# Turning the softmax weights as fp32r through a second tile at the same address

## The chip, the core and the metric

The kernel runs on one core of a Trainium2 chip. The metric is the device time of one execution in microseconds; the kernel before takes 804.97 us, the median of three runs from 804.18 to 805.74.

## What is computed

Three pieces follow each other. Attention with 2 batches, 8 heads, 576 rows and 64 columns a head keeps the 32 largest scores of every row. Its result, 1152 rows of 512, goes through a mixture of four experts, and that through a gated block:

```python
scores = scale * q @ k.T                       # 576 x 576 for each of 16 heads
kth = np.partition(scores, -32, axis=-1)[..., -32:-31]
attn = softmax(np.where(scores >= kth, scores, -1e9))
x = (attn @ v) as 1152 x 512
out = sum(p[:, e:e + 1] * (relu(x @ w1[e]) @ w2[e]) for e in range(4))   # F = 1024
out = (out @ w_a) * (out @ w_b) @ w_out        # 1536 columns between
```

## The kernel before

The rows are cut into nine tiles of 128 rows (eight of whole blocks, and one, MIX, of the 64 rows left over in each batch). The tiles form four groups of 1, 2, 3 and 3. Attention goes through 36 steps: for every group its four pairs of heads, and for every pair the tiles of the group. Steps 0 to 3 are of group 0, 4 to 11 of group 1, 12 to 23 of group 2 and 24 to 35 of group 3.

One step handles one tile and two heads. TensorE makes the scores; ScalarE moves them to SBUF (L905); VectorE finds the 32 largest of each row with eight MAX8 (L933) and six MATCH_REPLACE8 (L941), the replacements going into a buffer `e`. Then comes the softmax: GpSimd makes the ends (L958), ScalarE marks the kept scores (L964), GpSimd subtracts (L968), ScalarE takes the exponential (L972), GpSimd and VectorE make the reciprocal of the sum (L977 and L980), and ScalarE scales (L983). The softmax weights stand in `e`, of which there are three buffers, 1152 words each, inside the region `low`. In `weigh` (from L1015) TensorE turns them, four 128x128 transposes for one head and five for the other, all from the one line L573; ScalarE moves them to SBUF (L1050), and after the last tile of a pair they are multiplied with the values, from which `xs`, the experts' input, comes (L1084 and L1086).

Steps 0 to 23 turn `e` as float32. Steps 24 to 35 (the table `MOVED`) first copy both halves of `e` by a transfer into one of two buffers `er` of type fp32r in the region `big`, and turn those as fp32r.

The experts' work on a group needs all four pairs of that group. Its first layer has as moving operand 256 columns for group 1 and 384 for groups 2 and 3 (an experts' input of two or three tiles), its second layer 512. Weights are split in two fp32r parts by ScalarE (L1107) and GpSimd or VectorE (L1108). The sums of a group (L1205) are turned back in `replace` (transposes on L573 of float32, L1308, L1312).

All work is recorded as operations with an engine, an estimated duration, a priority key, the operations and the buffers that it waits for. A planner (`Plan.best`) simulates 42 orders from its own table of durations and keeps one; the instructions are then written out engine by engine in that order. Each engine runs its own instructions strictly in that order, so one instruction that waits holds up all that stand behind it on its engine. A changed duration, wait or buffer anywhere lets the planner place everything anew.

Of the kernel before, what the change touches and what calls it, by code (L numbers as in the profile page):

```python
# [9 lines left out]
F32 = mybir.dt.float32  # L10
F32R = mybir.dt.float32r
# [18 lines left out]
AHEAD = 2.4  # L30
OPERANDS = 3.0
STORED, STORE_AT, STORE_KEY = 3, 10, 2.5
MOVED = (*range(24,36),)

# [4 lines left out]
class Slots:  # L39
# [10 lines left out]
    def tile(self, need=0.0):  # L50
        t = Buffer(self, need)
        self.queue.append(t)
        return t
# [23 lines left out]
class Buffer:  # L77
    def __init__(self, slots, need):
        self.slots, self.need, self.slot, self.users = slots, need, None, 0

    @property
    def ap(self):
        a = self.slots.aps[self.slot]
        return a[0][a[1]] if isinstance(a, tuple) else a


class Op:
# [296 lines left out]
TURN_R, TURN_F, TOP, REPLACE = 88, 109, 662, 732  # L384
# [18 lines left out]
def body(tc, q, k, v, probs, w1, w2, wa, wb, wo, out):  # L403
    nc = tc.nc

    wa, wb, wo = (w.bitcast(U32) for w in (wa, wb, wo))
    B, H, S, D = q.shape
    E, DM, F = w1.shape
# [3 lines left out]
    M4 = S // 128  # L412
    MAIN = M4 * 128
# [7 lines left out]
    sb = stack.enter_context(tc.tile_pool(name="sb", bufs=1))  # L421
# [36 lines left out]
    identr = const("identr", [128, 128], F32R)  # L458
    ident = identr.bitcast(F32)
# [13 lines left out]
    big = Region("big", 10752, F32R)  # L473
# [8 lines left out]
    big.at = 0  # L482
    ers = big.slots("er", 2, 2 * S)
    ers.rank = 0.5
    mid = Region("mid", 4 * 2048 + 5 * 768, F32)
    wides = mid.slots("wide", WIDE, 2048)
    mid.again(F32R)
# [4 lines left out]
    first_ = Region("lowa", 4 * 2 * S + 4 * S, F32)  # L492
    pts = first_.slots("pt", 4, 2 * S)
    ss = first_.slots("s", 4, S)
    low = Region("low", 9228 + 3 * DM, F32)
    kraws = low.slots("kraw", 2, 2 * M4 * D)
    vts = low.slots("vt", 4, 2 * M4 * D)
    qraws = low.slots("qraw", 1, 2 * 3 * D)
    es = low.slots("e", 3, 2 * S)
    m8s = low.slots("m8", 2, 2 * TOPK)  # L500
    endss = low.slots("ends", 2, 4)
    sumss = low.slots("sums", 2, 2)
    hfs = low.slots("hf", 2, 512)
    krraws = kraws
    low.at = 9228
    yps = low.slots("yp", 1, DM)
    pws = low.slots("pw", 1, 1024)
    low.again()
    low.at = 9228
    ys = low.slots("y", 1, 3 * DM)  # L510

    first_.again(F32R)
# [3 lines left out]
    raw.again()  # L516
    ress = [raw.slots("res", 8, DM)]
    low.again()
    ress.append(low.slots("res2", 1, DM))
    draws = low.slots("draw", 2, 1024)  # L520
    dcs = low.slots("dc", 2, 512)
    vvs = low.slots("vv", 2, 2048)
    tps = [low.slots("tp", 2, 4 * 320), rest.slots("tpr", 1, 4 * 320)]
    taken_ = []
    ydone, ahead = {}, {}

# [36 lines left out]
    def gpsimd(hold, emit, key, after, tiles, lag=55):  # L563
        return plan.add("POOL", hold, emit, key, after, tiles, lag=lag, port=True)

    def tensor(hold, emit, key, after, tiles):
        return plan.add("PE", hold, emit, key, after, tiles, lag=165)
# [2 lines left out]
        nc.tensor.matmul(out, l, r, **kw)  # L570

    def tr(out, a, i):
        nc.tensor.transpose(out, a, i)  # L573

    def token_rows(t, rows):

# [22 lines left out]
    ready = gpsimd(1900, consts, -1e6, (), ())  # L599
# [417 lines left out]
    def weigh(pair, i, ed, n):  # L1017
# [15 lines left out]
        ke = -3000 if fast else -900  # L1033
        for j in range(2):

            at = atts.tile(kt)

            def turn(j=j, at=at):
                a = (at.ap if f is e else at.ap.bitcast(F32R)).rearrange("p b n -> p (b n)")
                if j:  # L1040
                    tr(a[:, MAIN - 128:MAIN], f.ap[:, MAIN:MAIN + 128], idt)
                for m in range(M4):
                    c0 = j * (S + REM) + m * 128
                    tr(a[:, j * MAIN + m * 128:j * MAIN + (m + 1) * 128], f.ap[:, c0:c0 + 128], idt)

            hold = (M4 + j) * TURN_F if f is e else 46 + (M4 + j - 2) * 85 + 64
# [575 lines left out]
```

## Time and profile before

| what | value |
|---|---|
| median of three runs | 804.97 us (804.18 to 805.74) |
| profiled execution, from first to last instruction | 802.1 us |
| TensorE matmul busy | 777.2 us, 97% |
| VectorE busy | 731.2 us, 91% |
| ScalarE busy | 528.6 us, 66% |
| GpSimd busy | 358.8 us, 45% |

The page gives the profiled execution no time but its span, which lies 2.9 us under the median of the runs. PE stands for TensorE's matmuls, DVE for VectorE, ACT for ScalarE, POOL for GpSimd, SP for the queue that issues transfers. A share of busy time is an average over stages with different limits, so the stages have to be read one by one; a PE that is shown busy is not always at its full rate, since the ends of matmuls are modelled.

### The profile page before, as it was taken

How to read it: one execution, taken by the hardware profiler on the slowest of the kernel's cores; microseconds unless marked ns; L12 is line 12 of the kernel's file. 1: busy time of each engine (PE TensorE's matmuls, PEld its weight loads, DVE VectorE, ACT ScalarE, POOL GpSimd, SP SyncE). 2: the span in 40 equal slices, each digit the busy share in tenths (PEclk: the TensorE clock that was granted, in tenths of full speed). 3: DMA queues.
4: the chain of work that ended last, by engine and by line, in shares of the span. 5: the costliest groups of instructions: out<-in, count | busy, mean ns of one | idle time of the engine just before them, and what ended most of it. 6: DMA issues, size and time to landing. Idle time of an engine off the chain costs nothing.

```text
span 802.1 us, 14540 instructions
## 1 busy us (share of the span) xinstructions
PE 777.2 (97%) x5221; PEld 701.1 (87%) x5221; DVE 731.2 (91%) x1430; ACT 528.6 (66%) x926; POOL 358.8 (45%) x323
## 2 busy tenths in 40 slices
PE   6699998999999999999999999999999999999998
PEld 5577776889999989999998898999888989899996
DVE  7999999999999999999996599898889998989655
ACT  5999888999898897877676566666545524242110
POOL 4645345899789856842111002332224334343120
PEclk7699999999999999999999999999999999999999
DMA  5987996867648575754444555888531322312013
GB/s 173 326 277 232 306 325 223 265 202 232 214 141 253 165 230 179 220 182 144 135 154 152 160 175 176 274 294 316 173 106 54 132 59 100 132 33 73 1 53 119
DMA packets 98008, 143.57 MB, mean 179 GB/s; under 512 B 11792, under 2 KB 66064, under 8 KB 96400
## 3 DMA queue, kind: packets, MB, share of 16 engines
q1 hardware_dynamic: 97936, 142.65, 55.5%
q8 instruction: 41, 0.67, 0.3%
q14 instruction: 31, 0.25, 0.1%
HBM read 117.46 MB, written 14.42 MB: 164 GB/s over the span
## 4 chain that ended last, share of the span: by engine, by line
PE 69%; DVE 17%; ACT 5%; DMA 3%; POOL 3%; issue 3%; SPq 0%; POOLq 0%; ACTq 0%; DVEq 0%
PE ps L570 66%; DVE low L933 7%; DVE low L941 6%; PE ps L573 3%; DMA mid<-in_moe_w_dram 1%; POOL low L968 1%; ACT mid_again L1107 1%; POOL mid_again L1108 1%; ACT lowa L905 1%; DMA big<-low 1%; DVE rest L1513 1%; ACT low L972 1%; DMA low<-in_q_dram 1%; POOL big L629 1%; DVE mid_again L1180 1%
## 5 line engine op out<-in xcount | busy, mean ns | idle before, releaser
L570 PE MATMUL ps<-mid_again 128*128 128x512 f32 x1092 | 263.0, 392 | 0.0
L570 PEld LDWEIGHTS ps<-mid_again 128*128 128x128 f32 x1092 | 201.2, 188 | 38.8
L570 PE MATMUL ps<-xs,mid_again 128*128 128x384 f32 (+1 forms) x1152 | 193.6, 320 | 0.5 <-DVE mid_again L1180 0.3
L570 PEld LDWEIGHTS ps<-xs,mid_again 128*128 128x128 f32 x1152 | 182.2, 189 | 3.2 <-issue 0.5
L933 DVE MAX8 low<-low 128x8 f32<-128x576 f32 x216 | 153.8, 745 | 0.0
L1424 POOL TENSOR_TENSOR low<-low 128x512 int32<-128x512 int32 x36 | 52.2, 1450 | 164.7 <-DVE low L1421 98.6
L1108 POOL TENSOR_TENSOR mid_again<-raw,mid_again 128x1024 fp32r<-128x1024 f32 x48 | 115.4, 2411 | 13.8 <-ACT mid_again L1107 8.2
L1107 ACT ACTIVATE mid_again<-raw 128x1024 fp32r<-128x1024 f32 x96 | 101.7, 1065 | 21.9 <-PE ps L570 14.3
L968 POOL TENSOR_TENSOR low<-lowa,low 128x576 f32<-128x576 f32 x72 | 102.0, 1433 | 28.0 <-ACT low L964 28.0
L941 DVE MATCH_REPLACE8 low<-low 128x576 f32<-128x576 f32 x144 | 106.0, 741 | 0.0
L570 PE MATMUL ps<-xs,big 128*128 128x320 f32 (+1 forms) x576 | 86.4, 297 | 0.2 <-DVE low L1513 0.2
L570 PEld LDWEIGHTS ps<-xs,big 128*128 128x128 f32 x576 | 80.3, 190 | 1.1 <-DVE low L1513 0.4
L1108 DVE TENSOR_TENSOR mid_again<-raw,mid_again 128x1024 fp32r<-128x1024 f32 x48 | 62.6, 1306 | 6.9 <-ACT mid_again L1107 6.9
L570 PE MATMUL ps<-lowa_again,big 128*128 128x320 f32 (+1 forms) x432 | 66.2, 296 | 0.9 <-ACT rest L1522 0.8
L1176 ACT ACTIVATE mid_again<-ps 128x384 fp32r<-128x384 f32 (+1 forms) x96 | 44.1, 461 | 30.1 <-PE ps L570 29.6
L570 PEld LDWEIGHTS ps<-lowa_again,big 128*128 128x128 f32 x432 | 60.7, 190 | 2.0 <-ACT rest L1522 1.1
L972 ACT ACTIVATE low<-low 128x576 f32<-128x576 f32 x72 | 56.2, 783 | 3.1 <-POOL low L968 3.0
L964 ACT ACTIVATE low<-lowa,low 128x576 f32<-128x576 f32 x72 | 53.9, 778 | 5.1 <-POOL low L958 5.1
L983 ACT ACTIVATE low<-low 128x576 f32<-128x576 f32 x72 | 53.2, 776 | 5.5 <-DVE low L980 5.4
L905 ACT ACTIVATE lowa<-ps 128x576 f32<-128x576 f32 x72 | 46.2, 655 | 15.9 <-POOL low L968 8.1
L1180 DVE SCALAR_TENSOR_TENSOR mid_again<-ps,mid_again 128x384 fp32r<-128x384 f32 (+1 forms) x96 | 48.1, 502 | 7.2 <-ACT mid_again L1176 6.9
L1516 POOL TENSOR_TENSOR low<-low 128x256 f32<-128x256 f32 (+1 forms) x30 | 28.5, 950 | 56.0 <-DVE low L1513 51.1
(122 smaller groups left out, 1189.2 us busy)
## 6 DMA issues: line engine op xcount, KB each, us to landing
raw<-in_moe_w_dram SPq DMA_DIRECT2D x116, 512.0 KB, 4.5
big<-kscr SPq DMA_DIRECT2D x20, 576.0 KB, 5.3
big<-low SPq DMA_DIRECT2D x24, 288.0 KB, 3.9
low<-in_v_dram SPq DMA_DIRECT2D x24, 256.0 KB, 4.2
low<-in_moe_w_b_dram SPq DMA_DIRECT2D x12, 512.0 KB, 3.6
low<-in_moe_w_a_dram SPq DMA_DIRECT2D x12, 512.0 KB, 3.5
low<-in_moe_w_out_dram SPq DMA_DIRECT2D x12, 512.0 KB, 4.3
wscr<-big SPq DMA_DIRECT2D x6, 1024.0 KB, 5.8
```

What stands on the lines that cost most here:

```text
L570: nc.tensor.matmul(out, l, r, **kw)
L905: S, lambda: nc.scalar.activation(s.ap.rearrange("p (c n) -> p c n", c=2), at.ap[:, :, 0:HALF], AF.Copy),
L933: 62 + 1.04 * width, lambda at=at, cs=cs: nc.vector.max(m8v()[:, x, cs], at()), key + 0.02 * r, [done],
L941: lambda at=at, cs=cs: nc.vector.match_replace(out=src[1](), in_to_replace=m8v()[:, x, cs], in_values=at(), imm_value=LOW),
L964: S, lambda x=x, s=s: nc.scalar.activation(ev(x), s.ap, AF.Relu, bias=endv()[:, x, 1:2], scale=-STEEP),
L968: pool_(S), lambda x=x, s=s: nc.gpsimd.tensor_tensor(ev(x), s.ap, ev(x), op=ALU.subtract), ks, [a], [s, ep]
L972: lambda x=x: nc.scalar.activation(ev(x), ev(x), AF.Exp, bias=endv()[:, x, 0:1], scale=scale, accum_out=sums.ap[:, x:x + 1]),
L983: S, lambda x=x: nc.scalar.activation(ev(x), ev(x), AF.Copy, scale=sums.ap[:, x:x + 1]),
L1107: hi = scalar(1024, lambda: nc.scalar.activation(u.ap[:, 0:1024], r.ap, AF.Copy), 500 + s, [ld], [u, r], sbuf=True)
L1108: sub = lambda eng: eng.tensor_tensor(u.ap[:, 1024:2048], r.ap, u.ap[:, 0:1024], op=ALU.subtract)
L1180: lambda h=h, p=p: nc.vector.scalar_tensor_tensor(h.ap[:, n:2 * n], p.ap[:, 0:n], 0.0, h.ap[:, 0:n], op0=ALU.max, op1=ALU.subtract),
L1424: return gpsimd(pool_(512), lambda: nc.gpsimd.tensor_tensor(t().bitcast(I32), fold(c.ap.bitcast(I32)), fold(lowv().bitcast(I32)), op=ALU.a ...
```

## The change

The three buffers `e` leave the region `low` and become tiles of their own, 1160 words each. Every step takes a new float32 tile in one of the three places. When the softmax weights are finished, `retype` takes a second tile of type fp32r at the same address and writes one word behind the weights with a GpSimd memset; that instruction stands for the producer of the fp32r tile. It waits for both L983 of the step, and the transposes, now fp32r in all 36 steps, wait for it. Before, the first head's transposes waited for the first L983 alone. The copies into `er` are gone, and so are those two buffers. Later users of the region `low` move to other offsets, and the buffers `draw` and `dc` of the last stage take the places of `e`. The planner's duration for a turn is now 280 and 365 ns instead of 436 and 545.

```diff
-MOVED = (*range(24,36),)
     def ap(self):
         a = self.slots.aps[self.slot]
+        if isinstance(a, Typed):
+            self.own = a.tile(F32) if self.own is None else self.own
+            return self.own[:, 0:a.words]
         return a[0][a[1]] if isinstance(a, tuple) else a
+class Typed:
+    def tile(self, dtype):
+        self.n += 1
+        return self.pool.tile([128, self.words + 8], dtype, name=f"{self.name}_{self.n}", tag=self.name)
-    ers = big.slots("er", 2, 2 * S)
-    low = Region("low", 9228 + 3 * DM, F32)
+    low = Region("low", 7180, F32)
-    es = low.slots("e", 3, 2 * S)
+    turns = [Typed(sb, f"e{i}", 2 * S) for i in range(3)]
+    es = Slots("e", turns, "e", [(i * 2 * S, (i + 1) * 2 * S) for i in range(3)])
...
-        f, idt = e, ident
-        if n in MOVED:
-
-            f, idt = ers.tile(n), identr
-            done = [load(
-                lambda j=j: f.ap[:, j * S:(j + 1) * S].bitcast(F32), lambda j=j: e.ap[:, j * S:(j + 1) * S], n + 0.1, [done[j]], [e, f], S * 512,
-            ) for j in range(2)]
+        turnable = []
+
+        def retype():
+            a = e.slots.aps[e.slot]
+            t_ = a.tile(F32R)
+            turnable[:] = t_, nc.gpsimd.memset(t_[:, a.words:a.words + 1].bitcast(F32), 0.0).ins
+
+        typed = gpsimd(90, retype, -4500, done, [e])
...
-            o = tensor(hold, turn, kt, [done[j], done[0], ready], [at, f])
+            o = tensor(46 + (M4 + j - 2) * 85 + 64, turn, kt, [typed, ready], [at, e])
```

What the planner made of it is shown at the softmax and the turn of step 23, the last step of group 2. Lines of the kernel after lie 19 further on for the steps' operations (L968 is L987, L980 is L999), 25 for the experts' (L1108 is L1133, L1312 is L1337). In the kernel after, the tiles of `e` carry their place and a serial number: step 23 is `e2_15_2673` as float32 and `e2_16_2942` as fp32r, step 24 is `e0_17_2815`, step 25 `e1_17_2910`.

GpSimd in the kernel before, from the ends of step 23 (L958) to the sums of its exponentials (L977):

```order
L958 TENSOR_TENSOR low<-low,facs 128x4
L1108 TENSOR_TENSOR mid_again<-raw,mid_again 128x1024
L968 TENSOR_TENSOR low<-lowa,low 128x576 x2
L1108 TENSOR_TENSOR mid_again<-raw,mid_again 128x1024
L977 TENSOR_SCALAR low<-low 128x2
```

GpSimd in the kernel after, from the memset of step 22 to the memset of step 23:

```order
L1048 MEMSET e1_16_2818 128x1
L977 TENSOR_TENSOR low_80<-low_80,facs_69 128x4
L1133 TENSOR_TENSOR mid_again_1275<-raw_78,mid_again_1275 128x1024
L987 TENSOR_TENSOR e2_15_2673<-lowa_79,e2_15_2673 128x576
L1133 TENSOR_TENSOR mid_again_1275<-raw_78,mid_again_1275 128x1024 x2
L987 TENSOR_TENSOR e2_15_2673<-lowa_79,e2_15_2673 128x576
L977 TENSOR_TENSOR low_80<-low_80,facs_69 128x4
L996 TENSOR_SCALAR low_80<-low_80 128x2
L987 TENSOR_TENSOR e0_17_2815<-lowa_79,e0_17_2815 128x576 x2
L1048 MEMSET e2_16_2942 128x1
```

Two more weight splits of 128x1024 stand between the two subtractions of step 23, the memset of step 22 stands ahead of its ends, and step 24's ends stand ahead of its sums.

VectorE in the kernel before, the last rows up to the reciprocal of step 23:

```order
L941 MATCH_REPLACE low<-low 128x576 x2
L933 MAX low<-low 128x8 x2
L941 MATCH_REPLACE low<-low 128x576
L1205 SCALAR_TENSOR_TENSOR low<-ps,pr,low 128x512
L941 MATCH_REPLACE low<-low 128x576
L980 RECIPROCAL low<-low 128x2
```

VectorE in the kernel after, the last rows up to the same reciprocal (L999):

```order
L1337 TENSOR_TENSOR xs_70<-ps_81,xs_70 128x2x256
L952 MAX low_80<-e0_17_2815 128x8
L952 MAX low_80<-lowa_79 128x8
L960 MATCH_REPLACE e1_17_2910<-low_80,lowa_79 128x576
L1337 TENSOR_TENSOR xs_70<-ps_81,xs_70 128x2x256
L952 MAX low_80<-lowa_79 128x8
L952 MAX low_80<-e1_17_2910 128x8
L960 MATCH_REPLACE e1_17_2910<-low_80,lowa_79 128x576
L960 MATCH_REPLACE e1_17_2910<-low_80,e1_17_2910 128x576
L999 RECIPROCAL low_80<-low_80 128x2
```

Before, step 24 was not yet through when the reciprocal came; after, step 24 is through and three replacements of step 25 and both L1312 of group 1 stand ahead of it.

TensorE in the kernel before around the turn of step 23 (the nine transposes from `low`):

```order
L570 MATMUL ps<-mid_again 128x512 x6
L570 MATMUL ps<-big 128x288 x8
L570 MATMUL ps<-mid_again 128x512 x18
L570 MATMUL ps<-xs,mid_again 128x384 x6
L573 MATMUL ps<-identr,low 128x128 x9
L570 MATMUL ps<-xs,mid_again 128x384 x6
L570 MATMUL ps<-big,qm 128x288 x8
```

TensorE in the kernel after around the same turn (`e2_16_2942`); the eight transposes from `low_80` are those of group 1's sums:

```order
L589 MATMUL ps_81<-mid_again_1275 128x512 x15
L592 MATMUL ps_81<-identr_65,e1_16_2818 128x128 x9
L589 MATMUL ps_81<-mid_again_1275 128x512 x6
L589 MATMUL ps_81<-big_76 128x288 x8
L589 MATMUL ps_81<-xs_70,mid_again_1275 128x384 x18
L592 MATMUL ps_81<-identr_65,low_80 128x128 x8
L589 MATMUL ps_81<-xs_70,mid_again_1275 128x384 x9
L592 MATMUL ps_81<-identr_65,e2_16_2942 128x128 x9
L589 MATMUL ps_81<-big_76,qm_68 128x288 x8
```

Of group 2's first layer 27 matmuls of 384 columns stand ahead of the turn instead of 6, and the eight transposes of group 1's sums, which stood behind it, stand ahead of it; all else ahead of the turn is the same in both kernels.

## Rows read from the trace of the kernel before

**Rows 1.** The page: busy time and share of the span by engine.

```profile
PE 777.2 (97%) x5221; PEld 701.1 (87%) x5221; DVE 731.2 (91%) x1430; ACT 528.6 (66%) x926; POOL 358.8 (45%) x323
```

**Rows 2.** Busy time by stretch: stretch, length, PE, PEld, DVE, ACT, POOL (instructions), clock, DMA.

```profile
60.00:135.00 75.00, 72.23 (x531) 56.33 (x531) 74.90 (x168) 65.92 (x123) 34.44 (x39) 1.00 0.87 275
160.00:285.00 125.00, 123.58 (x980) 113.15 (x979) 124.18 (x271) 114.21 (x212) 110.22 (x81) 1.00 0.67 206
285.00:420.00 135.00, 135.00 (x952) 124.19 (x953) 132.77 (x262) 105.46 (x182) 61.45 (x52) 1.00 0.54 170
420.00:802.00 382.00, 376.86 (x2258) 346.86 (x2256) 318.77 (x559) 171.57 (x274) 101.53 (x88) 1.00 0.41 137
```

**Rows 3.** The chain that ended last, 255 to 300 us: start, us, what.

```profile
270.61 0.66 DVE low L1205
...
280.90 1.46 DVE low L941 x2
...
284.15 0.69 DVE xs L1312
...
285.54 7.02 PE ps L570 x36
```

**Rows 4.** Timeline of TensorE at turns: start, us, engine, line, op, tiles, count.

```profile
87.81 1.15 PE L573 MATMUL ps<-identr,low 128*128 128x128 f32 x9
88.79 0.39 PE L570 MATMUL ps<-xf,raw 128*128 128x128 f32 x2
...
205.02 1.15 PE L573 MATMUL ps<-identr,low 128*128 128x128 f32 x9
205.92 1.40 PE L570 MATMUL ps<-mid_again 128*128 128x512 f32 x5
...
337.50 0.89 PE L573 MATMUL ps<-identr,big 128*128 128x128 f32 x9
338.23 1.16 PE L570 MATMUL ps<-mid_again 128*128 128x512 f32 x4
```

**Rows 5.** Timeline of TensorE, 268 to 293 us: step 23's turn, group 1's transposes.

```profile
273.61 1.15 PE L573 MATMUL ps<-identr,low 128*128 128x128 f32 x9
...
284.88 0.66 PE L573 MATMUL ps<-identr,low 128*128 128x128 f32 x4 [0.57 <-DVE xs L1312]
285.34 4.45 PE L570 MATMUL ps<-xs,mid_again 128*128 128x384 f32 x24
```

**Rows 6.** Timeline of GpSimd in step 23's softmax.

```profile
261.79 0.20 POOL L958 TENSOR_TENSOR low<-low,facs 128x4 f32<-128x4 f32 x1 [0.56 <-PE ps L570]
262.22 2.41 POOL L1108 TENSOR_TENSOR mid_again<-raw,mid_again 128x1024 fp32r<-128x1024 f32 x1 [0.24 <-ACT mid_again L1107]
264.58 2.82 POOL L968 TENSOR_TENSOR low<-lowa,low 128x576 f32<-128x576 f32 x2
```

**Rows 7.** Timeline of VectorE: last MAX8 and reciprocal of step 23.

```profile
260.23 1.41 DVE L933 MAX8 low<-low 128x8 f32<-128x576 f32 x2
...
271.91 0.15 DVE L980 RECIPROCAL low<-low 128x2 f32<-128x2 f32 x1
```

**Rows 8.** Instructions of one line: ns of one, min/median/max, and when.

```profile
L596 POOL MEMSET facs<- x1: 101/101/101, 2.1 to 2.1; 128x2 f32 x1
```

**Rows 9.** Last copy into `er` and the turn behind it: transfers page, chain, TensorE's timeline.

```profile
big<-low SPq DMA_DIRECT2D x24, 288.0 KB, 3.9
437.01 5.27 DMA big<-low
442.33 0.63 PE L573 MATMUL ps<-identr,big 128*128 128x128 f32 x5 [0.16 <-DMA big<-low]
```

**Rows 10.** Granted clock by stretch, and a wait that left it alone (columns as in rows 2).

```profile
20.00:30.00 10.00, 5.87 (x28) 5.11 (x29) 10.00 (x22) 9.41 (x22) 6.28 (x8) 0.50 0.90 281
130.00:140.00 10.00, 7.66 (x63) 5.24 (x63) 10.00 (x22) 8.11 (x13) 6.84 (x6) 1.00 0.53 171
135.06 0.66 PE L573 MATMUL ps<-identr,low 128*128 128x128 f32 x4 [2.35 <-ACT low L983]
```

More of the change, by code (lines that the diff above doesn't have):

```diff
@@ L79, in __init__ @@
         self.slots, self.need, self.slot, self.users = slots, need, None, 0
+        self.own = None
     @property
@@ L83, in ap, with __init__, __getitem__ @@
         a = self.slots.aps[self.slot]
+        if isinstance(a, Typed):
+            self.own = a.tile(F32) if self.own is None else self.own
+            return self.own[:, 0:a.words]
         return a[0][a[1]] if isinstance(a, tuple) else a
+class Typed:
+    def __init__(self, pool, name, words):
+        self.pool, self.name, self.words, self.n, self.last = pool, name, words, 0, None
+    def tile(self, dtype):
+        self.n += 1
+        return self.pool.tile([128, self.words + 8], dtype, name=f"{self.name}_{self.n}", tag=self.name)
+    def __getitem__(self, span):
+        if self.last is None:
+            self.last = self.tile(F32)
+        return self.last[:, span[0]:span[1]]
 class Op:
@@ L481, in body @@
     qts = big.slots("qt", 1, 2 * 3 * 128)
-    big.at = 0
-    ers = big.slots("er", 2, 2 * S)
-    ers.rank = 0.5
     mid = Region("mid", 4 * 2048 + 5 * 768, F32)
@@ L498, in body @@
     qraws = low.slots("qraw", 1, 2 * 3 * D)
-    es = low.slots("e", 3, 2 * S)
+    turns = [Typed(sb, f"e{i}", 2 * S) for i in range(3)]
+    es = Slots("e", turns, "e", [(i * 2 * S, (i + 1) * 2 * S) for i in range(3)])
+    es.rank = 0
     m8s = low.slots("m8", 2, 2 * TOPK)
@@ L504, in body @@
     krraws = kraws
-    low.at = 9228
+    low.at = 5644
     yps = low.slots("yp", 1, DM)
@@ L508, in body @@
     low.again()
-    low.at = 9228
+    low.at = 5644
     ys = low.slots("y", 1, 3 * DM)
@@ L518, in body @@
     low.again()
-    ress.append(low.slots("res2", 1, DM))
-    draws = low.slots("draw", 2, 1024)
-    dcs = low.slots("dc", 2, 512)
+    draws = Slots("draw", [(turns[i], (0, 1024)) for i in range(2)], "e", [(i * 2 * S, i * 2 * S + 1024) for i in range(2)])
+    dcs = Slots("dc", [(turns[2], (i * 512, (i + 1) * 512)) for i in range(2)], "e", [(4 * S + i * 512, 4 * S + (i + 1) * 512) for i in range(2)])
+    draws.rank = dcs.rank = 1
     vvs = low.slots("vv", 2, 2048)
     tps = [low.slots("tp", 2, 4 * 320), rest.slots("tpr", 1, 4 * 320)]
+    ress.append(low.slots("res2", 1, DM))
     taken_ = []
@@ L572, in tr @@
     def tr(out, a, i):
-        nc.tensor.transpose(out, a, i)
+        return nc.tensor.transpose(out, a, i)
     def token_rows(t, rows):
@@ L1023, in weigh @@
         (e, done), p, ptd = ed, pts.tile(n), []
-        f, idt = e, ident
-        if n in MOVED:
-            f, idt = ers.tile(n), identr
-            done = [load(
-                lambda j=j: f.ap[:, j * S:(j + 1) * S].bitcast(F32), lambda j=j: e.ap[:, j * S:(j + 1) * S], n + 0.1, [done[j]], [e, f], S * 512,
-            ) for j in range(2)]
+        turnable = []
[4 more added lines that the diff above has]
+        typed = gpsimd(90, retype, -4500, done, [e])
+        typed.port = False
         fast = n in HURRIED or n in SOONER
@@ L1038, in turn @@
             def turn(j=j, at=at):
-                a = (at.ap if f is e else at.ap.bitcast(F32R)).rearrange("p b n -> p (b n)")
+                a = at.ap.bitcast(F32R).rearrange("p b n -> p (b n)")
+                f, by = turnable
+                made = []
                 if j:
-                    tr(a[:, MAIN - 128:MAIN], f.ap[:, MAIN:MAIN + 128], idt)
+                    made.append(tr(a[:, MAIN - 128:MAIN], f[:, MAIN:MAIN + 128], identr))
                 for m in range(M4):
                     c0 = j * (S + REM) + m * 128
-                    tr(a[:, j * MAIN + m * 128:j * MAIN + (m + 1) * 128], f.ap[:, c0:c0 + 128], idt)
-            hold = (M4 + j) * TURN_F if f is e else 46 + (M4 + j - 2) * 85 + 64
-            o = tensor(hold, turn, kt, [done[j], done[0], ready], [at, f])
+                    made.append(tr(a[:, j * MAIN + m * 128:j * MAIN + (m + 1) * 128], f[:, c0:c0 + 128], identr))
+                tc.add_manual_dep(
+                    made[0].ins, by.name, mybir.DependencyInfo(mybir.DependencyClass.Sync, mybir.DependencyReason.DATA), reason="the tile's new type"
+                )
+            o = tensor(46 + (M4 + j - 2) * 85 + 64, turn, kt, [typed, ready], [at, e])
             w = MAIN + j * 128
```

## The prediction

> **What bounds the kernel now.** I read the profile from the whole to the stage. The page's first part says that TensorE is busy 97% of a span of 802.1 us and VectorE 91% [rows 1]: with 25 us of idle time on TensorE, work taken from it could shorten the kernel, if it is TensorE that the end waits for where the work is taken. So the next view is busy time by stretch [rows 2]. From 60 to 135 us VectorE is busy 74.90 of 75 us, from 160 to 285 us 124.18 of 125. It does top-8 searches and replacements there without a pause, and these set the pace at which steps are finished. TensorE is nearly full too, but has 2.8 and 1.4 us of idle time in the same stretches. From 285 to 420 us TensorE has no idle time at all, 135.00 of 135. Where does the pace change hands? The chain of work that ended last answers it [rows 3]: it runs along VectorE's searches up to the L1312 at 284.15 us, and goes over to TensorE at 284.88, to stay there but for short pieces. That is the border between groups 1 and 2. TensorE has finished what it can do for group 1, and group 2's experts need step 23, the last of their attention.
>
> So there are two stages. **Ahead of 285 us** the border is reached when VectorE has got through step 23, and time saved on TensorE becomes waiting. **Behind it** every microsecond of TensorE counts, but the turns there (steps 24 to 35) are fp32r already.
>
> **What the change takes off TensorE.** Nine float32 transposes take 0.90 us to the start of the next matmul (205.02 to 205.92), nine fp32r ones 0.73 (337.50 to 338.23) [rows 4]: 0.17 a step. Among float32 matmuls nine take 0.98 us (87.81 to 88.79) [rows 4], 0.25 over the fp32r row. For the 24 steps concerned that is 24 x 0.17 = 4.1 us, or 24 x 0.25 = 6.0. All of it lies ahead of the border. The wait of 2.35 us for an L983 at 135.06 us [rows 10] is the same situation one group earlier: there too the turn came later than TensorE could have taken it.
>
> The pages would have promised more. The Trainium skill, "FP8 and Floating Point Precision", section "TensorE Precision Notes", gives true float32 four passes through the array. By it a turn's transposes would fall to a quarter, and 24 x 0.90 x 3/4 = 16 us would go. The trace does not show that for transposes, whose rows stand at 0.90 and 0.73, and the measurement decides.
>
> **What goes with the transfers.** The 24 copies of 288 KB took 3.9 us each, the last one 5.27 us in the chain, but TensorE stood idle only 0.16 us for it [rows 9]; the others lay beside experts' matmuls in a stretch where TensorE never paused [rows 2]. I take 0.2 us. If the cover were gone it would be some 4 us for each of 12 steps; nothing in the order takes it away, since TensorE has group 2's matmuls to do all the while.
>
> **What is added.** 36 memsets of one word. The only small ones of the trace took 0.10 us [rows 8], so GpSimd gets 36 x 0.1 = 3.6 us; the bounds are 0 for one hidden and 2.41 us, a weight split, for one that must let that run out ahead of it [rows 6]. GpSimd is busy 110.22 of 125 us ahead of the border [rows 2], so the turn of a step will often wait for a split. A step's turn is not waited for in most cases; TensorE takes other work. The memset also waits for both L983, and behind it GpSimd's queue holds, in 13 of 36 places, the ends of the next step (L958). At step 23 that is the case. I take 0.1 to 0.8 us for the wait there: 0.1 for the memset, the rest for the second L983, for which the first head's turn did not wait before.
>
> **What is moved** decides. At step 23 GpSimd ran L958, one split and both subtractions in 5.6 us (261.79 to 267.40) [rows 6]. In the new order two more splits of 2.41 us stand between the subtractions, 4.8 us more. VectorE's own order follows that: ahead of step 23's reciprocal (271.91) [rows 7] now stand five more MAX8, three more replacements, one more L1205 and both L1312. Two MAX8 take 1.41 us [rows 7], two replacements 1.46, an L1205 0.66, an L1312 0.69 [rows 3]: 3.5 + 2.2 + 0.7 + 1.4 = 7.8 us; the 1.41 counts an overlap, so I take 7.5. VectorE cannot make this up, having no idle time there, and the order on an engine is fixed. The turn of step 23 began at 273.61, 1.7 us behind its reciprocal, so it should now begin near 281.
>
> TensorE gets work for this time: 21 matmuls of 384 columns that stood behind the turn, at 4.45 / 24 = 0.185 us (counting an overlap, so 0.18) [rows 5], 3.8 us; and the eight transposes of group 1's sums, two of the runs of 0.46 us (284.88 to 285.34) [rows 5], 0.9 us. Together 4.7. The rest of the 7.5 us, 2.8, is lost for good, because what is behind the turn is the same in kind and number but for these 4.7 us, and TensorE is the bound from there on. TensorE itself should be seen idle longer than 2.8 us around the border, by what it saved on the turns of steps 12 to 23 (12 x 0.17 = 2 us) and the 0.57 us below.
>
> **The sum,** against the profiled span of 802.1: +7.5 for the reciprocal of step 23, -4.7 for the work moved ahead of its turn, +0.1 to +0.8 for memset and second half (0.5 taken), -0.57 for the wait for L1312 at 284.88 [rows 5], which now falls in the longer wait, -0.2 for the transfers: 802.1 + 2.5 = 804.6. The saving on the turns stands at nothing in it. The median of the runs lies 2.9 us over the span; put on it, the same sum gives 804.97 + 2.5 = **807.5 us**. The memset between its ends (0 and 2.41) moves this from 807.0 to 809.4; the 5.1 us that TensorE idles behind 420 us [rows 2] may come out a microsecond otherwise in a new order. So the forecast's own range is 806.6 to 809.5.
>
> **Rivals.** First, *the saving counts*: VectorE passes step 23 no later than before, by gaps that the row of 124.18 out of 125 does not show, and TensorE's 4.1 to 6.0 us go through: 799.0 to 800.9. Against it speak the chain up to 284.15 and the missing idle time on VectorE.
>
> Second, *no difference*: the late step 23 is real, but the waits behind the border shrink (5.1 us of idle time are there [rows 2]) or VectorE's two L1205 and L1312, done earlier, save a wait later on: 2.5 less 1 to 4 us, 803.4 to 806.6. For it speaks that only TensorE's idle time is at stake, against it that most of it lies at the end, where the order is the same.
>
> Third, *the clock falls at the border*. TensorE would be idle some 5 us within 9, in two or three pieces with the eight transposes between. The trace holds both levels: at 130 to 140 us, with a wait of 2.35 us in one piece, the granted clock stayed at 1.00, that is 2.4 GHz; at 20 to 30 us, where TensorE worked in short pieces between waits from the start on, it stood at 0.50, 1.2 GHz [rows 10]. Had the clock fallen for 4 to 8 us of matmuls, half of that would be lost, 2 to 4 us on top: 809.5 to 811.5. The Trainium skill, "TensorE: Matmul & The Clock Gate", part 1 on the HAM clock gate, says that idleness takes the clock down to half and that sustained work is needed to bring it back; by that rule this case would be the likely one if the wait came in one piece; the row at 130 us agrees only in that its wait was too short to show it.
>
> **Chances.** Forecast 0.5, no difference 0.25, clock 0.13, saving counts 0.12. A difference under about 0.2% (1.6 us) cannot be told from none, so faster means below 803.4 and slower above 806.6: faster 0.12, same 0.25, slower 0.63. The range takes in the second case from 803.4 and the third nearly to its end: 803.2 to 811.2, leaving out the first and a little on top.
>
> **What would show it.** In the profile after: turns of nine at about 0.73 us; step 23's reciprocal near 279 to 280 us and its turn near 281; TensorE idle 4 to 6 us between 270 and 282 us where it was idle under 1; a chain on VectorE up to this turn and on TensorE behind it; POOL memsets of 0.1 us. Wrong would be the reading if the turn came by 275 us, if TensorE had idle time between 285 and 420 us, or if VectorE had gaps ahead of the border.

## The result, and the profile after

The changed kernel takes 813.88 us, the median of four runs from 812.25 to 815.7; the kernel before took 805.24 in the same comparison. The ratio is 1.011, with a 95% interval from 1.0093 to 1.0127: slower by 8.6 us. The prediction was 807.5 us with a range to 811.2, so the sign was right and the size too small. The profiled execution of the kernel after is the longest of the four: its own time is 815.7 us, its span 813.9. The two profiled executions lie 11.8 us apart, 3 us more than the medians; so much of what their traces differ by belongs to these two executions and not to the change.

The page, as in [rows 1]:

```profile
PE 780.2 (96%) x5221; PEld 702.1 (86%) x5221; DVE 735.3 (90%) x1430; ACT 526.3 (65%) x926; POOL 363.4 (45%) x359
```

TensorE stands idle 8.8 us longer than before (33.7 against 24.9, span less busy time), and its busy time has not fallen, though 24 turns are shorter. Where the idle time lies shows in the stretches of [rows 2]:

```profile
60.00:135.00 75.00, 71.88 (x539) 56.11 (x534) 73.65 (x163) 64.37 (x120) 35.65 (x45) 1.00 0.88 280
160.00:285.00 125.00, 119.97 (x919) 108.96 (x917) 123.72 (x270) 112.67 (x206) 111.27 (x91) 0.99 0.64 201
285.00:420.00 135.00, 133.63 (x986) 123.21 (x987) 132.45 (x264) 106.60 (x190) 65.05 (x68) 0.97 0.41 126
420.00:802.00 382.00, 378.93 (x2270) 349.62 (x2270) 322.23 (x561) 174.43 (x279) 102.16 (x89) 1.00 0.39 131
```

From 160 to 285 us TensorE is busy 3.6 us less than in [rows 2]. VectorE, which had 0.1 us of gaps between 60 and 135 us, now has 1.35. Between those two stretches lies the border of groups 0 and 1; here the row of before and that of after:

```profile
135.00:160.00 25.00, 24.94 (x186) 21.46 (x187) 25.00 (x55) 23.13 (x43) 20.97 (x18) 1.00 0.85 259
...
135.00:160.00 25.00, 23.85 (x164) 19.26 (x165) 23.73 (x53) 20.89 (x39) 19.62 (x18) 0.93 0.78 222
```

VectorE loses 1.3 us there too, and the clock column says 0.93. This loss is not the order's. Run e3 below has the same order on every engine, apart from transposes that it adds behind 275 us, and in its trace the row reads

```profile
135.00:160.00 25.00, 23.97 (x176) 19.87 (x177) 25.00 (x56) 22.04 (x39) 20.38 (x18) 1.00 0.83 250
```

Summed over all gaps between its instructions up to 270 us, VectorE stood idle 9.0 us, against 5.4 before and 7.5 in e3. Beside waits at the start, which both kernels have, its longest up to 270 us are for ScalarE's move of the scores (L924) and, at 141 us in the slow stretch, for TensorE (in order: total, times, longest):

```profile
DVE low L952 <- ACT lowa L924: 2.0, 4, 1.2
DVE low L1410 <- PE ps L589: 1.3, 1, 1.3
```

In the kernel before the scores' move held VectorE up once, for 0.6 us.

Then the border of groups 1 and 2, TensorE's timeline, against [rows 5]. The turn of step 22 comes first (nine transposes in 0.71 us, 270.19 to 270.90, against [rows 4]); the turn of step 23 comes at 286.20, not at 273.61:

```profile
270.19 0.88 PE L592 MATMUL ps<-identr,e 128*128 128x128 f32 x9
270.90 1.62 PE L589 MATMUL ps<-mid_again 128*128 128x512 f32 x6
...
278.57 0.66 PE L592 MATMUL ps<-identr,low 128*128 128x128 f32 x4 [1.41 <-DVE xs L1337]
281.35 2.68 PE L589 MATMUL ps<-xs,mid_again 128*128 128x384 f32 x9 [2.12 <-DVE xs L1337]
286.20 1.38 PE L592 MATMUL ps<-identr,e 128*128 128x128 f32 x9 [2.17 <-POOL e L1048]
```

The reciprocal of step 23 stands at 283.98, where [rows 7] have 271.91; the last MAX8 of that step starts at 266.72, where it started at 260.9 before:

```profile
266.72 0.76 DVE L952 MAX8 low<-e 128x8 f32<-128x576 f32 x1
...
283.98 0.16 DVE L999 RECIPROCAL low<-low 128x2 f32<-128x2 f32 x1
```

What the turn waited for last is read from the chain, against [rows 3] (start, us, what):

```profile
274.57 4.22 POOL mid_again L1133 x2
278.80 1.37 POOL e L987
...
280.83 0.76 ACT e L991 x2
...
283.79 0.87 ACT e L991 x2
284.66 1.34 ACT e L1002 x2
...
286.05 0.11 POOL e L1048
...
286.20 0.77 PE ps L592 x4
```

The chain goes over GpSimd and ScalarE: two weight splits between step 23's two subtractions, then its second exponential, then an exponential of step 24 ahead of step 23's L1002 on ScalarE, the memset, the turn. In [rows 3] it went along VectorE. But the chain shows only what came last, here by 0.5 us: the reciprocal was done at 284.14, and ScalarE was free for the L1002 at 284.66. The reciprocal itself waited for VectorE. Its input was there when GpSimd's L996 ended, at 281.89, and VectorE, which from 262 to 284 us stood idle for 0.04 us (the second row: stretch, length, VectorE's busy time, clock, DMA), came to it 2.1 us later:

```profile
281.68 0.21 POOL L996 TENSOR_SCALAR low<-low 128x2 f32<-128x2 f32 x1 [1.37 <-ACT e L991]
262.00:284.00 22.00, 21.96 (x48) 0.96 0.57 172
```

GpSimd's timeline, against [rows 6], shows the splits:

```profile
270.31 2.41 POOL L1133 TENSOR_TENSOR mid_again<-raw,mid_again 128x1024 fp32r<-128x1024 f32 x1 [0.62 <-ACT mid_again L1132]
272.68 1.44 POOL L987 TENSOR_TENSOR e<-lowa,e 128x576 f32<-128x576 f32 x1
274.08 4.72 POOL L1133 TENSOR_TENSOR mid_again<-raw,mid_again 128x1024 fp32r<-128x1024 f32 x2
278.76 1.40 POOL L987 TENSOR_TENSOR e<-lowa,e 128x576 f32<-128x576 f32 x1
```

The memsets themselves are short, as in [rows 8], but GpSimd stands idle in front of 16 of them (us, times):

```profile
L1048 POOL MEMSET e<- x36: 88/98/115, 29.9 to 438.4; 128x1 f32 x36
...
  ACT e L1002: 34.0, 16
```

And the clock, which in [rows 10] stayed at 1.00 in the wait of that trace, falls to 0.50 behind TensorE's waits:

```profile
280.00:285.00 5.00, 2.68 (x9) 2.17 (x9) 5.00 (x11) 3.94 (x8) 3.18 (x5) 0.71 0.32 102
285.00:290.00 5.00, 3.75 (x19) 3.28 (x21) 4.75 (x11) 3.05 (x6) 0.54 (x4) 0.50 0.00 0
```

Where TensorE falls back is seen when the columns of its matmuls are counted in both traces. The kernel before has done 27% of them at 271.8 us, and the kernel after is then 0.7 us behind; at 30% (295.1 us) it is 10.6 behind, at 70% (582 us) 9.1, and from 78% (642 us) on 11.5. Nearly all is lost at the border. Another 2 us go at 625 and 652 us, where TensorE waits twice for an addition of the gated block on VectorE (0.2 us in all in the kernel before):

```profile
PE ps L589 <- DVE low L1538: 2.2, 2, 1.4
```

### The profile page after: what moved, and what is told of

Its sections match the earlier page's. It is cut to its first block, busy times and chain, and to the rows that moved or that the text cites. A ratio compares the mean times of both kernels' runs of the same rounds, so it can differ in the third digit from the quotient of the medians.

```text
span 813.9 us, 14483 instructions
## 1 busy us (share of the span) xinstructions
PE 780.2 (96%) x5221; PEld 702.1 (86%) x5221; DVE 735.3 (90%) x1430; ACT 526.3 (65%) x926; POOL 363.4 (45%) x359
## 4 chain that ended last, share of the span: by engine, by line
PE 79%; DVE 8%; ACT 7%; POOL 2%; issue 2%; DMA 2%; POOLq 0%; SPq 0%; ACTq 0%; DVEq 0%
PE ps L589 75%; PE ps L592 3%; DVE low L952 3%; DVE e L960 3%; ACT mid_again L1132 1%; ACT e L983 1%; ACT e L1002 1%; DMA big<-big 1%; DMA low<-in_q_dram 1%; ACT e L991 1%; POOL mid_again L1133 1%; POOL e L987 1%; ACT lowa L924 1%; ACT lowa L1075 0%; ACT big L644 0%
## 5 line engine op out<-in xcount | busy, mean ns | idle before, releaser
L952 DVE MAX8 low<-e 128x8 f32<-128x576 f32 x216 | 155.5, 757 | 0.1
L1449 POOL TENSOR_TENSOR low<-e,e 128x512 int32<-128x512 int32 x36 | 53.5, 1486 | 160.1 <-DVE e L1446 99.2
L1133 POOL TENSOR_TENSOR mid_again<-raw,mid_again 128x1024 fp32r<-128x1024 f32 x48 | 115.1, 2408 | 15.5 <-ACT mid_again L1132 13.8
L987 POOL TENSOR_TENSOR e<-lowa,e 128x576 f32<-128x576 f32 x72 | 102.9, 1448 | 21.6 <-ACT e L983 21.5
L960 DVE MATCH_REPLACE8 e<-low,e 128x576 f32<-128x576 f32 x144 | 107.1, 753 | 0.0
L1133 DVE TENSOR_TENSOR mid_again<-raw,mid_again 128x1024 fp32r<-128x1024 f32 x48 | 60.1, 1258 | 10.4 <-ACT mid_again L1132 10.2
L991 ACT ACTIVATE e<-e,low 128x576 f32<-128x576 f32 x72 | 56.3, 784 | 3.8 <-POOL e L987 3.7
L1205 DVE SCALAR_TENSOR_TENSOR mid_again<-ps,mid_again 128x384 fp32r<-128x384 f32 (+1 forms) x96 | 48.7, 509 | 9.8 <-ACT mid_again L1201 9.3
L1002 ACT ACTIVATE e<-e,low 128x576 f32<-128x576 f32 x72 | 52.7, 781 | 6.9 <-DVE low L999 6.8
L983 ACT ACTIVATE e<-lowa,low 128x576 f32<-128x576 f32 x72 | 53.4, 779 | 5.0 <-POOL low L977 4.5
L924 ACT ACTIVATE lowa<-ps 128x576 f32<-128x576 f32 x72 | 45.8, 656 | 13.4 <-PE ps L589 7.5
L952 DVE MAX8 low<-lowa 128x8 f32<-128x576 f32 x70 | 51.1, 756 | 3.3 <-ACT lowa L924 3.2
```

The costliest lines, as they stand in the source:

```text
L924: S, lambda: nc.scalar.activation(s.ap.rearrange("p (c n) -> p c n", c=2), at.ap[:, :, 0:HALF], AF.Copy),
L952: 62 + 1.04 * width, lambda at=at, cs=cs: nc.vector.max(m8v()[:, x, cs], at()), key + 0.02 * r, [done],
L960: lambda at=at, cs=cs: nc.vector.match_replace(out=src[1](), in_to_replace=m8v()[:, x, cs], in_values=at(), imm_value=LOW),
L983: S, lambda x=x, s=s: nc.scalar.activation(ev(x), s.ap, AF.Relu, bias=endv()[:, x, 1:2], scale=-STEEP),
L987: pool_(S), lambda x=x, s=s: nc.gpsimd.tensor_tensor(ev(x), s.ap, ev(x), op=ALU.subtract), ks, [a], [s, ep]
L991: lambda x=x: nc.scalar.activation(ev(x), ev(x), AF.Exp, bias=endv()[:, x, 0:1], scale=scale, accum_out=sums.ap[:, x:x + 1]),
```

## The experiments

All were timed against runs of the kernel before on the same chip, which stood at 804.2 to 805.0 us.

| run | what | us | ratio to before, 95% |
|---|---|---|---|
| e1 | changed operations, old order | 825.30 | 1.0240 to 1.0273 |
| e2 | changed operations, another new order | 808.40 | 1.0035 to 1.0059 |
| e3 | after, TensorE kept busy at the border | 813.84 | 1.0095 to 1.0125 |
| e4 | weights written as fp32r, new order | 803.52 | 0.9976 to 0.9996 |
| e5 | the same, old order | 806.04 | 1.0012 to 1.0034 |
| e6 | one word written by ScalarE, old order | 813.14 | 1.0096 to 1.0128 |
| e7 | after, step 23 moved forward by hand | 815.86 | 1.0129 to 1.0158 |
| e8 | one word written by ScalarE, new order | 805.57 | 1.0010 to 1.0032 |
| e9 | the same, order of the kernel after | 816.42 | 1.0124 to 1.0163 |
| e10 | as e4, another order | 802.83 | 0.9963 to 0.9987 |
| e11 | kernel before, another order | 804.20 | 0.9986 to 1.0011 |
| e12 | kernel before, step 23 made late | 817.76 | 1.0134 to 1.0179 |
| e13 | after, re-planned from 258 us, step 23 first | 808.22 | 1.0025 to 1.0052 |
| e14 | after, re-planned from 258 us | 811.92 | 1.0055 to 1.0098 |

**Is the shorter turn worth anything? (e5, e4)** Both write the softmax weights straight into a fourth buffer, which fits into room unused in the region `low`:

```diff
-    ers = big.slots("er", 2, 2 * S)
+    turnable = Region("turnable", 1 * 2 * S, F32R)
+    fs = turnable.slots("f", 1, 2 * S)
...
-                S, lambda x=x: nc.scalar.activation(ev(x), ev(x), AF.Copy, scale=sums.ap[:, x:x + 1]),
+                S, lambda x=x: nc.scalar.activation(turned.ap[:, x * S:(x + 1) * S], ev(x), AF.Copy, scale=sums.ap[:, x:x + 1]),
```

e5 takes the order of the kernel before as a table of places, which the planner must follow on every engine:

```diff
+TOLD = (
...
+)
         def pick(engine):
+            line = told.get(engine)
+            if not line or line[-1].left or line[-1].at > now:
+                return None
...
+            return line.pop()
```

> As e4 (L983 writes the weights as fp32r into a fourth buffer, no memsets, no copies, lowest bits of the weights left out), but in the order of the kernel before, engine by engine. What differs from the kernel before is then hardly more than the turns of 24 steps at 0.73 instead of 0.90 to 0.98 us. If time saved on TensorE ahead of the border becomes waiting, as I predicted: 803.4 to 805.0 us against 804.4. If the saving counts: 798.4 to 800.3 us (4.1 to 6.0 less).

> From the kernel before: L983 writes the softmax weights straight into a fourth buffer of type fp32r (it lies in room that stood unused in the region low), which all 36 turns read. No memset, no copies, and the first half's turn waits for the first L983 alone; e is free at L983. The weights are rounded as they are written, so their lowest bits are left out. The planner makes a new order of it. If memset and the wait for both halves made the loss, this has the turns' saving without them: 799 to 803 us. If a new order costs some us either way, whatever its operations, it can land from 801 to 810 us.

e5 took 806.04, 1.0 over before and outside both its ranges. In it a turn goes from 205.73 to 206.46, 0.73 us where [rows 4] have 0.90, and step 23's turn begins at 274.29 where [rows 5] have 273.61:

```profile
205.73 0.89 PE L675 MATMUL ps<-identr,turnable 128*128 128x128 f32 x9
206.46 0.93 PE L672 MATMUL ps<-mid_again 128*128 128x512 f32 x3
...
274.29 0.88 PE L675 MATMUL ps<-identr,turnable 128*128 128x128 f32 x9
```

The two traces have the same order, so TensorE can be compared instruction by instruction: e5 lies 0.8 us ahead at 129 us, 0.8 behind at 139, and from there to 289 us between 0.5 and 0.9 behind. What it loses between 129 and 139 us goes with a granted clock that fell in this execution, behind a wait of 2.5 us at the place of the 2.35 us in [rows 10]:

```profile
135.00:140.00 5.00, 5.00 (x36) 3.69 (x37) 5.00 (x11) 3.15 (x6) 4.11 (x4) 0.66 0.61 204
```

From 139 to 289 us twelve shorter turns move it by nothing. The saving ahead of the border is waiting, as predicted. Behind 289 us the trace of e5 falls back by some 2 us more; why, and why its median is 1.0 us over before, stays open. e4, with a new order, is 0.8 us faster than before; that is not the saving either, as e5 shows.

**What do the memset and the wait for both halves cost when nothing else moves? (e1, e6)** e1 is the kernel after with the old order as such a table, each memset just ahead of its turn. e6 lets ScalarE write the one word:

```diff
-            turnable[:] = t_, nc.gpsimd.memset(t_[:, a.words:a.words + 1].bitcast(F32), 0.0).ins
+            turnable[:] = t_, nc.scalar.activation(t_[:, a.words:a.words + 1], facs[:, 0, 0:1], AF.Copy).ins
-        typed = gpsimd(90, retype, -4500, done, [e])
+        scaled = done[1].emit
+        done[1].emit = lambda: (scaled(), retype())
```

> The changed operations (own tiles for e, fp32r turns, memsets, no copies) in the order of the kernel before, engine by engine; each memset stands on GpSimd just ahead of its turn. If the order that the planner made anew is the cause, VectorE goes through its work as before and step 23's turn begins at 273 to 276 us: 802 to 807 us. If the wait for the second L983 and the memset is the cause (0.6 to 0.9 us at each of the 24 turns that stood right behind the first half), the loss stays or grows: 811 to 825 us, with TensorE's idle time ahead of the turns.

> As e1 (the changed operations in the order of the kernel before), but the one word behind the weights is written by ScalarE right behind the second L983, and GpSimd has no memset. The first half's turn still waits for both halves. In e1 GpSimd stood idle 29.7 us ahead of 16 memsets, and TensorE waited 26.1 us for 26 of them. If the memset's place in GpSimd's queue makes the loss of 21 us, most of it goes: 804 to 809 us. If the wait for the second half makes it (some 0.7 us at 26 turns), it stays: 815 to 823 us.

825.30 and 813.14 us, a loss of 20.9 and 8.1 against the runs of before beside each. TensorE's waits for the weights to be turned (total, times, longest), in the kernel before, in e1, in e6, in e5 and in the kernel after:

```profile
PE ps L573 <- ACT low L983: 5.8, 4, 2.3
```

```profile
PE ps L693 <- POOL e L1149: 26.1, 26, 3.8
```

```profile
PE ps L695 <- ACT e L1151: 16.8, 19, 2.8
```

```profile
PE ps L675 <- ACT turnable L1086: 6.0, 4, 2.5
```

```profile
PE ps L592 <- POOL e L1048: 6.4, 4, 2.2
```

In the old order, then, the memset, at the place that I gave it in GpSimd's queue, costs some 13 us (e1 less e6). The other 7 (e6 less e5) are the wait for both halves, ScalarE's 0.2 us for the word and the different places of the tiles, which no run tells apart. Neither theory held alone: e6 lies between its two ranges. This is the cost that the planner had to arrange itself around; with a new order both edits cost less (the kernel after, and e8 below).

**Is it the memsets or the order? (e8, e9, e2, e11)** e8 is e6's edit with an order made anew. e9 is the same edit in the order of the kernel after, so that only the memsets are gone from GpSimd. e2 and e11 are the kernels after and before with `random.Random(r + 3000)` and `random.Random(r + 10000)` in the planner.

> The kernel after with the one word written by ScalarE right behind the second L983 instead of a memset on GpSimd; the planner makes its order anew. If the memset's place in GpSimd's queue was the cause of the loss: 802 to 806 us. If the wait for both halves, or the new places of the tiles: 809 to 815 us.

> The kernel after in its own order, engine by engine, but the 36 memsets are taken out of GpSimd's queue; ScalarE writes the one word right behind the second L983. The opposite of e6. If it is the waiting memsets in GpSimd's queue that cost time (34 us of idle time on GpSimd ahead of 16 of them in the kernel after), the time goes to 804 to 809 us. If it is the order that the planner made to fit them in (late step 23, VectorE's new order), it stays at 811 to 815 us.

> The kernel after with another start for the planner's random numbers and nothing else: the same operations, another order. If the order is the cause, this order costs something else: 803 to 810 us, at least 3 us from 813.9. If the operations themselves (memset, wait for both halves, tiles' places) are the cause, it stays at 812 to 816 us.

> The kernel before with another start for the planner's random numbers, and nothing else; it measures what an order alone is worth with the old operations. If the order kept before was a lucky one: 806 to 812 us. If orders of the same operations differ little there: 803 to 806.5 us, and then what e2 shows (5.4 us between two orders of the changed operations) comes from how the memsets lie in them.

e9 took 816.42: with every memset out of GpSimd's queue the loss is all there (12.2 us, even more than 8.6). VectorE still waits for the scores' move as in the kernel after (there 3.2 us in 6 waits over the whole run):

```profile
DVE low L1055 <- ACT lowa L1027: 3.4, 6, 1.2
```

Taking the waiting memsets out gives nothing back in this order. That they cost nothing in it is not shown, since e9 puts 36 words on ScalarE instead, for which the order was not made; but the loss stays with the order, and at the same place: TensorE is 1.8 us behind the kernel before at 27% of its columns and 11.5 at 30%. e8 says the same from the other side: with the word on ScalarE (36 writes of 203 ns) the planner finds an order that costs 0.6 us. e2 moves by some 5 us from the kernel after through the order alone, while e11 does not move (804.20 against 804.24). What e2 does lose, 4.0 us, it too loses at the border (1.4 us ahead at 27% of the columns, 5.1 behind at 30%). Orders of the old operations need not differ; of the changed ones, these two do.

**Where in the order? (e7, e12, e13, e14)** e7 puts step 23's operations back by hand on GpSimd, ScalarE, VectorE and TensorE in the table of the kernel after; e12 does the reverse to the kernel before. In both only such tables are changed.

> The kernel after in its own order but for step 23: the two splits go behind the second subtraction, step 23's second exponential, reciprocal and L983 stand ahead of step 24's last search and of step 25's, as in the kernel before, and its turn stands ahead of the last four transposes of group 1's sums. If the late step 23 is what costs time, as I predicted (2.5 us by my sum, up to the 9 us by which TensorE fell back at the border in the profile): turn at 277 to 281 us instead of 286.2 and 805 to 811.5 us. If VectorE's gaps ahead of the border cost it, and step 23 is late whatever its order: 812.5 to 815 us.

> The kernel before (float32 turns, copies, no memsets) in its own order, with step 23 alone put where the kernel after has it: two splits between its subtractions, five MAX8, three replacements, one L1205 and both L1312 ahead of its reciprocal, 27 instead of 6 matmuls of 384 columns and group 1's eight transposes ahead of its turn. It measures the term +2.5 us of my sum by itself. If my sum holds: 806.0 to 808.0 us against 804.5. If the late step costs what TensorE's waits at the border of the kernel after show (5.9 us of idle time in place of 0.6, and matmuls at half clock): 809 to 814 us; most of the change's loss then lies there. If other waits take it up: 803.5 to 805.5 us.

e7's turn came at 278.74, 7.5 us sooner (by 2.0 it was ahead already at step 22's turn, 268.19 against 270.19), and the kernel was no faster (815.86, outside both its ranges):

```profile
278.74 0.97 PE L693 MATMUL ps<-identr,e 128*128 128x128 f32 x9 [3.57 <-POOL e L1149]
...
281.69 3.25 PE L690 MATMUL ps<-xs,mid_again 128*128 128x384 f32 x9 [1.41 <-DVE xs L1438]
...
294.49 1.01 PE L690 MATMUL ps<-xs,mid_again 128*128 128x384 f32 x2 [1.52 <-DVE xs L1212]
```

TensorE's waits went over to the `xs` of groups 1 and 2, whose subtractions I had left where they were on VectorE. e12 gave 817.76, above all that was expected, but it overstates: in it ScalarE stands still behind a move of group 1's sums that the hand-made order puts ahead of an exponential,

```profile
276.11 0.60 ACT L1408 ACTIVATE xs<-ps 128x512 fp32r<-128x512 f32 x1 [6.50 <-PE ps L673]
```

and VectorE with it. Both are inconclusive on the size: pulling one step out of an order leaves others stuck. So in e13 and e14 the order of the kernel after is kept up to 258 us of the plan, and the planner makes the rest; e13 also puts step 23 first:

```diff
-HURRIED, SOONER = (99,), (99,)
+HURRIED, SOONER = (99,), (99, 23)
```

> The kernel after, its own order kept engine by engine up to 258 us of the plan; from there planned anew, with step 23's softmax and turn ahead of all else on GpSimd, ScalarE, VectorE and TensorE. Its second subtraction then stands ahead of the two splits. e14 is the same without the preference. If the late step 23 costs the time: turn near 281 us instead of 286.2, and 806 to 811 us, at least 3 us under e14. If it is lost ahead of 258 us (VectorE's gaps) or behind 290 us: within 1.5 us of e14.

> The kernel after, its own order kept up to 258 us of the plan, then planned anew without any preference. The order it gives is that of the kernel after on all engines up to 279 us and on TensorE up to 294 us, so step 23 is as late as there; behind it differs. If the late step 23 costs the time: 812 to 815.5 us. If what stands behind the border costs it: 805 to 810 us.

808.22 and 811.92. TensorE's timeline of e13, then of e14:

```profile
277.94 0.66 PE L642 MATMUL ps<-identr,low 128*128 128x128 f32 x4 [1.79 <-DVE xs L1387]
280.01 1.84 PE L639 MATMUL ps<-xs,mid_again 128*128 128x384 f32 x9 [1.41 <-DVE xs L1387]
281.78 0.97 PE L642 MATMUL ps<-identr,e 128*128 128x128 f32 x9
```

```profile
280.87 2.28 PE L639 MATMUL ps<-xs,mid_again 128*128 128x384 f32 x9 [2.12 <-DVE xs L1387]
284.83 1.38 PE L642 MATMUL ps<-identr,e 128*128 128x128 f32 x9 [1.68 <-POOL e L1098]
```

With step 23 first its turn comes 3 us sooner and waits for nothing, and the kernel gains 3.7 us. That is the share of step 23's late place in the order. 3.4 us remain in e13. In it VectorE ends step 23's last MAX8 at 267.5 us, as in the kernel after (261.6 before), so most of the 3.4 should come from what lies ahead of 258 us. This share is argued, not shown: e13's own order loses something too, since VectorE stands still behind its reciprocal:

```profile
285.36 1.42 DVE L1002 MAX8 low<-lowa 128x8 f32<-128x576 f32 x2 [5.34 <-ACT lowa L974]
```

The last 1 to 2 us, from e14 to the kernel after, are not clear of the intervals; in the traces they are the two waits for L1538, which the kernel after, e3, e7 and e9 have and e14 has not (0.2 us in all). The intervals of e13 and e14 are 1 to 2 us to a side, and the parts are no better than that.

**The clock (e3).** 48 transposes of the identity fill three waits:

```diff
     for op in plan.best():
+        if op in border or op.engine == "PE" and fills == 1:
+            fills += 1
+            for i in range(12 if fills == 1 else 18):
+                tr(ps[:, 5, 0:128], ident, ident)
         op.emit()
```

> The kernel after, its order untouched; in the three waits of TensorE at 277 to 286 us it makes 12, 18 and 18 more transposes of the identity into a free bank (0.11 us each at full clock, 5.2 us in 5.7 us of waits). If the clock's fall at 282 us costs what my third rival said (2 to 4 us), the granted clock stays at 1.00 there and the time is 810 to 812 us. If the clock costs little because VectorE sets the time there, 813 to 815 us. If the fillers run over into real work, up to 1 us more.

The fillers overwrite part of one head's scores of step 25, so only the time counts. The granted clock stays at 1.00:

```profile
280.00:285.00 5.00, 5.00 (x44) 4.97 (x41) 5.00 (x13) 4.12 (x8) 3.13 (x4) 1.00 0.09 33
285.00:290.00 5.00, 4.74 (x66) 4.43 (x66) 4.82 (x11) 3.92 (x8) 0.51 (x3) 1.00 0.09 16
```

but the median is where it was, at 813.84, with an interval of some 1.3 us to either side. One run of e3 had a mean clock of 0.998 over its whole span, so it can have spent at most 4 us at half clock in all, and took 813.71. The two traces do differ behind the border: from step 22's turn (270.19 in the kernel after, 268.59 in e3) to these rows they take 24.3 and 22.2 us:

```profile
294.45 1.33 PE L589 MATMUL ps<-big,qm 128*128 128x288 f32 x8
```

```profile
290.76 1.33 PE L590 MATMUL ps<-big,qm 128*128 128x288 f32 x8
```

The clock falls, and its price at the border lies between nothing, as in the medians, and the 2 us of these two executions.

**A version that beats both (e10).** e4 with `SEED = 42000`:

> As e4 (weights written as fp32r by L983 into a fourth buffer, their lowest bits left out; no memset, no copies), with another start for the planner's random numbers, one that its own table rates 2 us better than e4's. If an order's worth on the chip follows that rating: 800 to 802.5 us. If orders differ by chance: 802.5 to 807 us. Turns' saving itself is worth nothing by e5.

802.83 us, 0.25% under before and 11 us under the kernel after. It has no memset, no copy and no wait for the second half.

## Why the prediction was right in sign and wrong in size

**The saving at nothing: right.** e5 has the shorter turns and keeps the old order; between 139 and 289 us TensorE gains nothing on the kernel before. The Trainium skill, "FP8 and Floating Point Precision", section "TensorE Precision Notes", counts four passes for true float32, by which 16 us would have left TensorE; the rows of 0.90 and 0.73 us speak against that for transposes. The Trainium skill, "TensorE: Matmul & The Clock Gate", section "Terms", names a transpose mode that is four times faster for FP32, which would fit these rows; that it is what runs here no run shows.

**The memset's price: right for the instruction, wrong for the queue.** 98 ns each, as taken. "A step's turn is not waited for in most cases" is true of the kernel after (6.4 us in 4 waits), but because everything had been placed anew around it; in the old order 26 turns wait 26 us (e1). I priced the memset inside an order that was already its consequence, and so saw its cost only at one step.

**"VectorE cannot make this up, having no idle time there": the step that failed.** For this step I took VectorE as coming to step 23 no later than before, and my sum had 0 for it. In the kernel after, step 23's last MAX8 starts 5.8 us later (266.72 against 260.9, the second of the two at 260.23 in [rows 7]). 3.6 us of that are further gaps, of which 1.4 are waits for the scores' move and 1.3 the slow clock at 141 us; 2.2 us are work that the new order puts ahead, three more moves of the experts' first layer (L1205) above all. In e3, where the clock did not fall, the same order is 4.2 us late. The order showed the rows; I compared them at three places and not up to the border.

**The late step 23: right place, right instructions, term too small.** The reciprocal came 12.1 us late (predicted 7.5). 5.8 us of it are the late start above. The rest, 6.2 us, is VectorE's own way from the last MAX8 to the reciprocal, 16.5 us against 10.3, without a gap to speak of: the eleven instructions that I added up, less four moves of the experts' first layer (L1180) that now went ahead and that I had not taken off. The two splits do stand in the chain, which goes over GpSimd and ScalarE; that way ended 0.5 us behind VectorE's, so the two are nearly level, and one alone would hardly have freed the turn. TensorE's idle time at the border was rightly sized (1.41, 2.12 and 2.17 us, predicted 4 to 6).

Put into the prediction's own sum, the reciprocal's 12.1 us in place of 7.5 give 7.1 us instead of 2.5, that is 812.1; with e3's 10.5 (its reciprocal comes at 282.39) it is 810.5. This is an estimate from single executions. The waits for L1538, 2.0 us more than before, bring it to 812.5 to 814.1, and 813.9 was measured. For e14 (reciprocal at 282.77, and no such waits) the same sum gives 810.9; it took 811.92.

**No idle time on TensorE from 285 to 420 us: wrong.** 1.4 us are missing there; the wait for the turn lies across 285. VectorE's gaps ahead of the border, another of the signs that I had named, came too.

**The rivals.** The saving did not count, and "no difference" did not come. The third, the falling clock, happened as described, at half level from 282 us for 10 us. The rule of the Trainium skill, "TensorE: Matmul & The Clock Gate", part 1, that idleness halves the clock agrees with that row. Its price of 2 to 4 us is not in the medians: e3 holds the clock and gains nothing; only the two traces leave room for 2 us. That the time of 813.9 lies above that rival's 809.5 to 811.5 has the other reasons.

Put together, of 8.6 us: 3.7 for step 23's late place (e13 against e14), about 3.4 for VectorE's late arrival there (what e13 leaves, not isolated by a run), 1 to 2 behind the border, against the 2.5 us predicted. What stays open is why the planner's best order with the memsets is bad where one with ScalarE's word is good; e2 says that part of it is the draw.

## What to carry to other kernels

An instruction that exists only to mark data as ready is better put on the engine that made the data: behind the second half on ScalarE it cost 0.6 us in the order made for it, in GpSimd's queue 8.6 and 4.0 in two such orders; in the old order the two cost 8.1 and 20.9. Better still, let that engine write the wanted type itself (e10). Where a planner sets the order, time a change once in the old order too: only then is it seen what the operations cost and what the new order does. And where the engine that sets the pace has no idle time, compare everything that stands ahead on it, up to the place that matters: a late start there comes on top of all that is counted at that place.

## What the runs showed that I had not expected

Half clock for 10 us right behind the border left the median where it was. At 135 to 140 us the clock falls in some executions and not in others of the same order (0.66 in the traces of the kernel after, e13 and e14, 1.00 in e3 and e7). ScalarE writes 576 columns as fp32r in the same 775 ns as float32, and a single word takes it 203 ns, twice GpSimd's 98. And two orders of the same operations lay some 5 us apart, while two of the kernel before lay 0.04 apart.
